# One attention and feed-forward block: K's and Q's weight blocks loaded together, in another order

## The chip, the cores and the metric

The kernel runs on one core of a Trainium2 chip. The metric is the time of the program on the device in microseconds (us): the median of 3 runs before the change. A profile of one execution stands beside it.

The engines are named as in the profile: PE is TensorE (matrix products), PEld its weight loads, DVE is VectorE, ACT is ScalarE, POOL is GpSimd, SP is SyncE. SP and ACT issue the DMAs of this kernel (SPq, ACTq).

## The reference

One input x of 2048 rows by 512 goes through a layer norm, and then through two branches whose results are added to x:

```python
def _A_ref(x, wqkv, wo):            # 32 heads of 16
    qkv = (x @ wqkv).reshape(B, S, 3, H, Dh).transpose(2, 0, 3, 1, 4)
    q, k, v = qkv[0], qkv[1], qkv[2]
    phi = lambda t: jnp.where(t > 0, t + 1, jnp.exp(t)) + 1e-6
    pq, pk = phi(q), phi(k)
    kv = jnp.einsum("bhsd,bhse->bhde", pk, v)
    z = jnp.einsum("bhsd->bhd", pk)
    num = jnp.einsum("bhqd,bhde->bhqe", pq, kv)
    den = jnp.einsum("bhqd,bhd->bhq", pq, z)[..., None] + 1e-6
    return (num / den).transpose(0, 2, 1, 3).reshape(B, S, D) @ wo

def _B_ref(x, w_gate, w_up, w_down):  # F = 1792
    return (silu(x @ w_gate) * (x @ w_up)) @ w_down

xn = layernorm(x)
return x + _A_ref(xn, A_wqkv, A_wo) + _B_ref(xn, B_w_gate, B_w_up, B_w_down)
```

All tensors are bfloat16. `A_wqkv` is 512 by 1536: in each row stand 512 columns for Q, then 512 for K, then 512 for V, that is 3 KB.

## The kernel before

The 2048 rows are 16 tiles of 128 (t = 0 to 15), and the 512 columns are four blocks of 128 (c = 0 to 3, `NDC`). A projection of one tile is four products that add into one PSUM bank, one for each block c; it needs x's tile transposed and block c of the weight matrix (128 rows, 512 columns, 128 KB).

The order of the work is written out by hand. `_Prog` keeps a list of operations for each engine in the order in which they are recorded, and puts a semaphore wait ahead of an operation only where another engine or a DMA has to be waited for. Each engine works through its list in order, and SP and ACT issue the DMAs in the order of their lists. Nothing is rearranged later.

The stages are:

1. **Start (about the first 11 us).** PE runs products on constants (`fill`, L271) until x tile 0 is there. For tiles 0 to 3, x less its mean (`xc_sb`) is transposed without waiting for the standard deviation, whose inverse is put in afterwards as a scale when ACT reads the product. VectorE makes the statistics (`bns`, L299, then `agg`, L302) and subtracts the mean (L380, L426); PE transposes (L410, L444; the transposes of tile 3 are a DMA, L435); ACT and VectorE copy the results into `xcT` (L419, L421, L456). Then `proj_part` (L499) makes one product of one block at a time for tiles 0 and 1, for K (`"wk"`) and Q (`"wq"`), and `proj_first` (L486) does two blocks at a time for tiles 2 and 3. ACT evacuates K with `first_ek` (L556, exp) and `first_pk` (L562, relu), and Q with `first_pq` (L574). GpSimd adds the two K parts of tile 0 (`feat_pool`, L581).
2. **K, Q and the state (to about 47 us).** For each further tile: K and Q projection (L472), then four products of `gtacc` (L624), which add pk's products with the normalised x into four banks.
3. **The feed-forward (to about 208 us).** 56 steps of gate and up products (L821), with the 16 output tiles (L1015, L1026) among them. An output tile is added to x on VectorE (L1039) and stored by SP (L1043).

Of the loads: `xload(eng, h, t0, n)` (L206) loads n tiles of x from tile t0, `wqkv_load` (L213) loads n blocks of one of the three matrices. The rows of the first `NLONE` = 6 tiles are taken as they stand (a tile is 128 consecutive rows); the other ten tiles share their rows so that partition p holds ten consecutive rows and two tiles are loaded as one piece of 2 KB a partition. The mapping also holds for the stores. A tile's rows of x and its rows of the output are the same, and no other step depends on which rows a tile has.

In the start `proj_part` is called in this order, where 0 and 1 are tiles, and the number behind the name is the block:

```python
# K: tile 0: blocks 0, 1, 3, 2; then tile 1: blocks 0, 1, 3, 2
# Q: tile 1: blocks 0, 1; tile 0: blocks 0, 1
#    (four transposes of tile 2)
# Q: block 2 of tile 0, of tile 1; block 3 of tile 0, of tile 1
```

Of the kernel before, what the change touches and what calls it, by code (L numbers as in the profile page):

```python
# [10 lines left out]
P = 128  # L11
S = 2048
D = 512
# [96 lines left out]
def bass_parallel_sum__linear_attn_block__swiglu_ffn__prompt_kernel(  # L110
# [12 lines left out]
    K = _Prog()  # L123
    pe, act, dve, pool, sp = nc.tensor, nc.scalar, nc.vector, nc.gpsimd, nc.sync
    bf, f32 = dt.bfloat16, dt.float32

    with contextlib.ExitStack() as es:
        E = es.enter_context

        def sb(name, shape, d=bf):  # L130
            return E(nc.sbuf_tensor(name, [P] + shape, d))
# [7 lines left out]
        wqkv_sb = sb("wqkv_sb", [NDC, 3 * D])  # L139
# [16 lines left out]
        warm = sb("warm", [1], f32)  # L156
# [35 lines left out]
        def bk(i):  # L192
            return ("bank", i)

        NLONE = 6

        def rows(v, t0, n):
            if t0 < NLONE:  # L200
                return v[t0 * P:(t0 + n) * P, :].rearrange("(t p) d -> p t d", p=P)
            return v[NLONE * P:, :].rearrange("(p t) d -> p t d", t=NT - NLONE)[:, t0 - NLONE:t0 - NLONE + n, :]

        def xload(eng, h, t0, n, after=()):
            K.dma(
                eng, lambda: h.dma_start(x_sb[:, t0:t0 + n, :], rows(xin, t0, n)),  # L206
                r=list(after), w=[("x", t0 + i) for i in range(n)],
            )

        def wqkv_load(eng, h, name, i, c0, n, after=()):  # L210
            K.dma(
                eng,
                lambda: h.dma_start(  # L213
                    wqkv_sb[:, c0:c0 + n, i * D:(i + 1) * D],
                    A_wqkv[c0 * P:(c0 + n) * P, i * D:(i + 1) * D].rearrange("(c p) f -> p c f", p=P),
                ),
                r=list(after), w=[(name, c) for c in range(c0, c0 + n)],
            )

        def wload(eng, h, name, dst, src):  # L220
# [28 lines left out]

        xload("sp", sp, 0, 1)  # L250
        wqkv_load("sp", sp, "wk", 1, 0, 2)
        wqkv_load("act", act, "wk", 1, 3, 1)
        wqkv_load("sp", sp, "wk", 1, 2, 1)
        xload("sp", sp, 2, 1)
        wqkv_load("sp", sp, "wq", 0, 0, 1)
        wqkv_load("sp", sp, "wq", 0, 1, 1)
        xload("sp", sp, 3, 1)
        wqkv_load("sp", sp, "wq", 0, 2, 1)
        wqkv_load("sp", sp, "wq", 0, 3, 1)
        xload("sp", sp, 4, 1)  # L260
        xload("sp", sp, 5, 1)
        xload("sp", sp, 6, 2)

        cw = nc.const_aps.tensor(1.0, (P, P), bf)
# [33 lines left out]
        def bns(t):  # L298
            K.op("dve", lambda: dve.bn_stats(stats[:, t, :], x_sb[:, t, :]), r=[("x", t)], w=[("st", t)])  # L299

        def agg(t):
            K.op("dve", lambda: dve.bn_aggr(mv[:, t, :], stats[:, t, :]), r=[("st", t)], w=[("mv", t)])  # L302
# [129 lines left out]
        def transpose_xc(t):  # L432
            K.dma(
                "sp",
                lambda: sp.dma_start_transpose(out=xcT[:, NDC * t:NDC * (t + 1), :], in_=xc_sb[:, t, :]),  # L435
                r=[("xc", t, 0), ("xc", t, 1)], w=[("xcT", t, c) for c in range(NDC)],
            )
# [43 lines left out]
        def proj_first(t, wname, h):  # L481
            lo, b = (D, kb(t)) if wname == "wk" else (0, qb(t))
            K.op(
                "pe",
                [
                    (lambda c=c: pe.matmul(  # L486
                        banks[b], xcT[:, NDC * t + c, :], wqkv_sb[:, c, lo:lo + D],
                        start=(c == 0), stop=(c == NDC - 1),
                    ))
                    for c in (2 * h, 2 * h + 1)  # L490
                ],
                r=[("xcT", t, i) for i in (2 * h, 2 * h + 1)] + [(wname, i) for i in (2 * h, 2 * h + 1)], w=[bk(b)],
            )

        def proj_part(t, wname, c, pos):
            lo, b = (D, kb(t)) if wname == "wk" else (0, qb(t))
            K.op(
                "pe",
                lambda: pe.matmul(  # L499
                    banks[b], xcT[:, NDC * t + c, :], wqkv_sb[:, c, lo:lo + D],  # L500
                    start=(pos == 0), stop=(pos == NDC - 1),
                ),
                r=[("xcT", t, c), (wname, c)], w=[bk(b)],
            )

        def kb(t):
            return 2 * (t % 2)

        def qb(t):
            return 2 * (t % 2) + 1  # L510
# [43 lines left out]
        def first_ek(t):  # L554
            K.op(
                "act", lambda: act.activation(ek[:, t % NE, :], banks[kb(t)], ACT.Exp, scale=rstd[:, t:t + 1]),  # L556
                r=[bk(kb(t)), ("rstd", t)], w=[("ek", t % NE)],
            )

        def first_pk(t):  # L560
            K.op(
                "act", lambda: act.activation(kpos[:, t % NE, :], banks[kb(t)], ACT.Relu, scale=rstd[:, t:t + 1]),  # L562
                r=[bk(kb(t)), ("rstd", t)], w=[("kpos", t % NE)],
            )
# [7 lines left out]
        def first_pq(t):  # L572
            K.op(
                "act", lambda: act.activation(pkq[:, t, 1, :], banks[qb(t)], ACT.Identity, scale=rstd[:, t:t + 1]),  # L574
                r=[bk(qb(t)), ("rstd", t)], w=[("pq", t)],
            )
# [96 lines left out]
        agg(3)  # L673
        proj_part(0, "wk", 0, 0)
        proj_part(0, "wk", 1, 1)
        proj_part(0, "wk", 3, 2)
        proj_part(0, "wk", 2, 3)
        first_ek(0)
        clip_k(0)
        xc_full(3)  # L680
        bns(4)
        proj_part(1, "wk", 0, 0)
        proj_part(1, "wk", 1, 1)
        proj_part(1, "wk", 3, 2)
        proj_part(1, "wk", 2, 3)
        proj_part(1, "wq", 0, 0)
        proj_part(1, "wq", 1, 1)
        transpose_xc(3)
        xload("sp", sp, 8, 2)
        xload("sp", sp, 10, 2)  # L690
        proj_part(0, "wq", 0, 0)
        proj_part(0, "wq", 1, 1)
        first_pk(0)
        tp_first(2, 0, 4)
        tc_first(2, 0, 4)
# [4 lines left out]
        agg(5)  # L700
        bns(6)
        agg(6)
        proj_part(0, "wq", 2, 2)
        proj_part(1, "wq", 2, 2)
        proj_part(0, "wq", 3, 3)
        first_pq(0)
        proj_part(1, "wq", 3, 3)
        proj_first(2, "wk", 0)
        proj_first(2, "wk", 1)
        eps_two(1, "pool")  # L710
# [413 lines left out]
```

## Time and profile before

| what | value |
|---|---|
| median of 3 runs | 210.15 us (209.99 to 210.45) |
| profiled execution | 210.88 us |
| its span, from the first instruction to the last | 209.6 us |
| PE busy | 206.9 us (99%) |
| DVE, ACT, POOL busy | 120.3, 71.3, 72.0 us |
| DMA traffic | 16.84 MB, mean 80 GB/s |

The profiled execution is one execution with the profiler on; times within it are microseconds from the start of its span. In the timeline a row gives the start, the length, the engine, the line, the operation with what it writes and reads, and how many instructions were merged. A row for a DMA on SPq or ACTq is the issuing of it, not the transfer. In brackets stands how long the engine had been idle, and what ended that. PE's products are pipelined: each is shown with its whole way through the array, so successive rows overlap.

### The profile page before, as it was taken

To read this page: it belongs to the slowest core of one execution; us is meant where nothing else is said; L and a number is where in the kernel's file an instruction comes from. 1 tells how busy PE (TensorE), PEld (TensorE's weight loads), DVE (VectorE), ACT (ScalarE), POOL (GpSimd) and SP (SyncE) were. 2 spreads that over 40 slices of the span, in tenths; PEclk is the share of its full clock that TensorE was granted. 3 is DMA by queue.
4 is the path that set the end of the run, shared out by engine and by line. 5 is a ranking of instruction groups with operands and counts; after the bars stand their busy time and mean duration, and the time that the engine had idled before them with its cause. 6 is when DMAs were issued, how large, how long until landed. Compare 5 with 4: busy or idle time off the path is not lost.

```text
span 209.6 us, 2822 instructions
## 1 busy us (share of the span) xinstructions
PE 206.9 (99%) x1014; PEld 94.5 (45%) x1014; DVE 120.3 (57%) x246; ACT 71.3 (34%) x126; POOL 72.0 (34%) x90
## 2 busy tenths in 40 slices
PE   8999999999999999999999999999999999999996
PEld 3444444444444444444444444444444444444444
DVE  4989989335465874637355746365556535374122
ACT  6686666976543331302122312213031213121000
POOL 3526977658032443223141422240424132221200
DMA  6763644697797021010101110102011010110101
GB/s 201 225 179 71 127 78 100 175 377 240 192 359 68 2 46 26 29 25 25 50 2 50 28 25 25 50 0 53 2 48 25 27 28 25 46 32 25 50 28 50
DMA packets 30287, 16.84 MB, mean 80 GB/s; under 512 B 20928, under 2 KB 29632, under 8 KB 30272
## 3 DMA queue, kind: packets, MB, share of 16 engines
q1 hardware_dynamic: 29984, 16.39, 29.9%
q10 hardware_dynamic: 288, 0.26, 0.4%
q8 instruction: 8, 0.13, 0.3%
q14 instruction: 7, 0.06, 0.1%
HBM read 9.70 MB, written 2.10 MB: 56 GB/s over the span
## 4 chain that ended last, share of the span: by engine, by line
PE 97%; DMA 1%; DVE 1%; issue 0%
PE psum L821 46%; PE psum L1026 23%; PE psum L472 10%; PE psum L1015 7%; PE psum L624 7%; PE psum L499 2%; PE psum L486 2%; DMA x_sb<-in_A_x_dram 1%; PE psum L444 0%; DVE stats L299 0%; PE psum L928 0%; PE psum L410 0%; PE psum L951 0%; DVE xc_sb L380 0%; DVE out_sb L1039 0%
## 5 line engine op out<-in xcount | busy, mean ns | idle before, releaser
L836 ACT ACTIVATE sg<-psum 128x512 bf16<-128x512 f32 x56 | 33.4, 598 | 106.0 <-PE psum L821 103.6
L821 PE MATMUL psum<-xnT,wg_sb 128*128 128x512 bf16 x224 | 57.5, 379 | 0.0
L821 PE MATMUL psum<-xnT,wu_sb 128*128 128x512 bf16 x224 | 57.5, 379 | 0.0
L970 POOL TENSOR_TENSOR prod<-pkq,zb 128x512 f32<-128x512 bf16 x16 | 18.6, 1161 | 55.9 <-DVE pkq L548 55.9
L821 PEld LDWEIGHTS psum<-xnT,wu_sb 128*128 128x128 bf16 x224 | 21.9, 98 | 26.4
L821 PEld LDWEIGHTS psum<-xnT,wg_sb 128*128 128x128 bf16 x224 | 21.7, 98 | 26.2 <-issue 0.2
L1039 DVE TENSOR_TENSOR out_sb<-psum,x_sb 128x512 bf16<-128x512 f32 (+2 forms) x17 | 11.2, 660 | 35.9 <-PE psum L1026 35.9
L994 POOL TENSOR_TENSOR pqn<-pkq,rden 128x512 bf16<-128x512 bf16 x16 | 16.9, 1055 | 36.6 <-DVE rden L988 36.6
L842 DVE TENSOR_TENSOR pkq<-psum,sg 128x512 bf16<-128x512 f32 x28 | 19.2, 686 | 17.1 <-PE psum L821 14.7
L842 DVE TENSOR_TENSOR xn_sb<-psum,sg 128x512 bf16<-128x512 f32 x28 | 18.8, 671 | 14.2 <-PE psum L821 13.6
L1026 PE MATMUL psum<-wd_sb,xn_sb 128*128 128x512 bf16 (+2 forms) x126 | 25.7, 355 | 0.0
L1026 PE MATMUL psum<-wd_sb,pkq 128*128 128x512 bf16 x112 | 25.5, 379 | 0.0
L472 PE MATMUL psum<-wqkv_sb,xnT 128*128 128x512 bf16 x96 | 22.5, 379 | 0.0
L616 POOL TENSOR_TENSOR zacc<-zacc,pkq 128x512 f32<-128x512 f32 x15 | 17.3, 1155 | 5.0 <-DVE ek L539 4.6
L1026 PEld LDWEIGHTS psum<-wd_sb,xn_sb 128*128 128x128 bf16 x126 | 11.8, 98 | 12.5
L1026 PEld LDWEIGHTS psum<-wd_sb,pkq 128*128 128x128 bf16 x112 | 11.0, 98 | 13.2
L1015 PE MATMUL psum<-m_sb,eq 128*128 128x512 bf16 (+2 forms) x68 | 16.6, 366 | 0.0
L624 PE MATMUL psum<-pkq,xn_sb 128*128 128x512 bf16 x64 | 15.9, 379 | 0.0
L472 PEld LDWEIGHTS psum<-wqkv_sb,xnT 128*128 128x128 bf16 x96 | 9.4, 98 | 11.3
L978 DVE TENSOR_REDUCE den<-prod 128x32 f32<-128x512 f32 x16 | 10.9, 683 | 5.9 <-POOL prod L970 5.9
L299 DVE BATCH_NORM_STATS2 stats<-x_sb 128x6 f32<-128x512 bf16 x16 | 10.9, 679 | 3.3 <-DMA x_sb<-in_A_x_dram 3.3
L548 DVE SCALAR_TENSOR_TENSOR pkq<-pkq,eq 128x512 bf16<-128x512 bf16 x16 | 11.1, 693 | 0.6
(73 smaller groups left out, 139.3 us busy)
## 6 DMA issues: line engine op xcount, KB each, us to landing
out_dram<-out_sb SPq DMA_DIRECT2D x15, 128.0 KB, 1.7
wg_sb<-in_B_w_gate_dram SPq DMA_DIRECT2D x2, 896.0 KB, 8.2
wu_sb<-in_B_w_up_dram SPq DMA_DIRECT2D x2, 896.0 KB, 6.4
wd_sb<-in_B_w_down_dram SPq DMA_DIRECT2D x1, 1792.0 KB, 11.1
x_sb<-in_A_x_dram SPq DMA_DIRECT2D x5, 256.0 KB, 3.0
x_sb<-in_A_x_dram SPq DMA_DIRECT2D x5, 128.0 KB, 3.2
wqkv_sb<-in_A_wqkv_dram SPq DMA_DIRECT2D x5, 128.0 KB, 3.4
wqkv_sb<-in_A_wqkv_dram SPq DMA_DIRECT2D x1, 512.0 KB, 8.4
```

Of the source, the lines that this page charges most:

```text
L472: (lambda c=c: pe.matmul(banks[b], xnT[:, c, t * P:(t + 1) * P], wqkv_sb[:, c, lo:lo + D], start=(c == 0), stop=(c == NDC - 1),))
L548: lambda: dve.scalar_tensor_tensor(out=dst, in0=src, scalar=0.0, in1=e, op0=ALU.max, op1=ALU.add,),
L616: lambda: pool.tensor_tensor(out=zacc[:, :], in0=zacc[:, :], in1=pk, op=ALU.add),
L624: (lambda c=c: pe.matmul(banks[4 + c], xn_sb[:, t, c * P:(c + 1) * P], pkq[:, t, 0, :], start=(t == 0), stop=(t == NT - 1),))
L821: (lambda c=c: pe.matmul(banks[b], w_sb[:, c, fc * P:(fc + 1) * P], xnT[:, c, C * 512:(C + 1) * 512], start=(c == 0), stop=(c == NDC - 1),))
L836: lambda: act.activation(sg[:, j % NSG, :], banks[gb], ACT.Silu),
L842: lambda: dve.tensor_tensor(out=hT(C, fc), in0=banks[ub], in1=sg[:, j % NSG, :], op=ALU.mult,),
L970: lambda: pool.tensor_tensor(out=p, in0=pkq[:, t, 1, :], in1=zb[:, :], op=ALU.mult),
L994: lambda: pool.tensor_tensor(out=pqn[:, t % NPN, :].rearrange("p (i g h e) -> p g i h e", i=NB, g=NG, e=DH), in0=pkq[:, t, 1, :].rearrange ...
L1015: (lambda g=g: pe.matmul(dst, pqnT(t)[:, g, :], m_sb[:, g, lo:hi], start=(g == 0), stop=False,))
L1026: (lambda fc=fc: pe.matmul(dst, hT(C, fc)[:, jj * P:(jj + 1) * P], wd_sb[:, fc, lo:hi], start=False, stop=(fc == NFC - 1),))
L1039: lambda: dve.tensor_tensor(out=o, in0=src, in1=x_sb[:, t, lo:hi], op=ALU.add),
```

## The change

- K's blocks 2 and 3 are no longer loaded alone. `qk_load` loads block c of Q and of K together: in each row of `A_wqkv` these are 1024 neighbouring columns, 2 KB. It is called for blocks 2 and 3.
- Q's blocks 0 and 1 come in one load, behind x tile 3.
- x tile 2 is issued on ACT rather than on SP. It waits for the warm-up activation (`warm`). K's block 3, which ACT issued, is now part of SP's second joint load.
- `NLONE` is 4: x tiles 4 and 5 come in one load of 2 KB pieces, and tiles 4 to 15 share their rows in twelves.
- The products of tiles 0 and 1 follow the new order of the blocks.

```diff
-        NLONE = 6
+        NLONE = 4
...
+        def qk_load(eng, h, c):
+            K.dma(
+                eng,
+                lambda: h.dma_start(wqkv_sb[:, c, 0:2 * D], A_wqkv[c * P:(c + 1) * P, 0:2 * D]),
+                w=[("wk", c), ("wq", c)],
+            )
...
         xload("sp", sp, 0, 1)
         wqkv_load("sp", sp, "wk", 1, 0, 2)
-        wqkv_load("act", act, "wk", 1, 3, 1)
-        wqkv_load("sp", sp, "wk", 1, 2, 1)
-        xload("sp", sp, 2, 1)
-        wqkv_load("sp", sp, "wq", 0, 0, 1)
-        wqkv_load("sp", sp, "wq", 0, 1, 1)
+        xload("act", act, 2, 1, [("warm",)])
+        qk_load("sp", sp, 2)
+        qk_load("sp", sp, 3)
         xload("sp", sp, 3, 1)
-        wqkv_load("sp", sp, "wq", 0, 2, 1)
-        wqkv_load("sp", sp, "wq", 0, 3, 1)
-        xload("sp", sp, 4, 1)
-        xload("sp", sp, 5, 1)
+        wqkv_load("sp", sp, "wq", 0, 0, 2)
+        xload("sp", sp, 4, 2)
         xload("sp", sp, 6, 2)
...
         proj_part(0, "wk", 0, 0)
         proj_part(0, "wk", 1, 1)
-        proj_part(0, "wk", 3, 2)
-        proj_part(0, "wk", 2, 3)
+        proj_part(0, "wk", 2, 2)
+        proj_part(1, "wk", 0, 0)
+        proj_part(1, "wk", 1, 1)
+        proj_part(0, "wk", 3, 3)
+        proj_part(1, "wk", 2, 2)
+        proj_part(1, "wk", 3, 3)
         first_ek(0)
         clip_k(0)
         xc_full(3)
         bns(4)
-        proj_part(1, "wk", 0, 0)
-        proj_part(1, "wk", 1, 1)
-        proj_part(1, "wk", 3, 2)
-        proj_part(1, "wk", 2, 3)
-        proj_part(1, "wq", 0, 0)
-        proj_part(1, "wq", 1, 1)
+        proj_part(0, "wq", 2, 0)
+        proj_part(0, "wq", 3, 1)
...
-        proj_part(0, "wq", 0, 0)
-        proj_part(0, "wq", 1, 1)
+        proj_part(1, "wq", 2, 0)
+        proj_part(1, "wq", 3, 1)
         first_pk(0)
...
-        proj_part(0, "wq", 2, 2)
-        proj_part(1, "wq", 2, 2)
-        proj_part(0, "wq", 3, 3)
+        proj_part(0, "wq", 0, 2)
+        proj_part(0, "wq", 1, 3)
+        proj_part(1, "wq", 0, 2)
         first_pq(0)
-        proj_part(1, "wq", 3, 3)
+        proj_part(1, "wq", 1, 3)
```

The last argument of `proj_part` is the product's place among its four (the first clears the bank, the last closes the sum).

## The prediction

> **What bounds the kernel now.** I read the page first, then TensorE's share by stage, then the chain of waits over the first 12 us, and last the timeline of that stretch. On the page:
>
> ```profile
> span 209.6 us, 2822 instructions
> ...
> PE 206.9 (99%) x1014; PEld 94.5 (45%) x1014; DVE 120.3 (57%) x246; ACT 71.3 (34%) x126; POOL 72.0 (34%) x90
> ...
> PE 97%; DMA 1%; DVE 1%; issue 0%
> ```
>
> The span is TensorE (PE) work. Busy time by windows (length, then busy time of PE, PEld and the others) says where it isn't:
>
> ```profile
> 11.20:47.60 36.40, 36.40 (x171) 16.51 (x169) 27.02 (x64) 26.16 (x48) 24.64 (x36) 1.00 0.63 163
> 47.60:207.80 160.20, 160.18 (x803) 73.45 (x801) 85.31 (x158) 37.65 (x63) 42.44 (x40) 1.00 0.21 53
> 207.80:209.60 1.80, 0.00 (x0) 0.00 (x0) 0.29 (x1) 0.00 (x0) 0.00 (x0) 1.00 0.25 73
> ```
>
> From 11.2 to 207.8 us PE is full: 0.02 us idle in 196.6. The last 1.8 us are the last store. So only the start is left, which is where the change works. The chain of waits there and PE's rows of the timeline (start, length):
>
> ```profile
> 0.80 2.15 DMA x_sb<-in_A_x_dram
> ...
> 4.26 0.40 PE psum L410 x2
> ```
> ```profile
> 5.09 3.52 PE L499 MATMUL psum<-wqkv_sb,xcT 128*128 128x512 bf16 x12
> 8.45 0.39 PE L444 MATMUL psum<-ident,xc_sb 128*128 128x128 bf16 x4
> 8.67 1.03 PE L499 MATMUL psum<-wqkv_sb,xcT 128*128 128x512 bf16 x4
> ```
>
> PE's first useful work, at 4.26, follows x tile 0 through VectorE; the change touches nothing on that path. From then on PE's rows follow one another without idle time: **no product waits for a weight block in this trace.** What is slow is the rate. Weight loads (PEld) inside the first twelve products:
>
> ```profile
> 5.95 0.15 PEld L499 LDWEIGHTS psum<-wqkv_sb,xcT 128*128 128x128 bf16 x1 [0.28 <-issue]
> 6.37 0.15 PEld L499 LDWEIGHTS psum<-wqkv_sb,xcT 128*128 128x128 bf16 x1 [0.27 <-issue]
> 6.72 1.39 PEld L499 LDWEIGHTS psum<-wqkv_sb,xcT 128*128 128x128 bf16 x7 [0.20 <-issue]
> ```
>
> Products start 0.42 us apart up to 6.37, 0.35 apart once, then 1.39 / 7 or about 0.2 apart (the twelve take 8.45 - 5.09 = 3.36). PE runs at half rate until about 6.6 us. Of twelve products 3.6 are at half rate and cost 3.6 x 0.21 = 0.77 us more than at full rate.
>
> **Where the weights stand against their use.** Issues on SP and ScalarE (SPq, ACTq), ScalarE's warm-up and the first copy of x tile 0 for PE, then the answers of the DMA view in narrow windows round single issues (KB, us from issue to landing):
>
> ```profile
> 1.10 0.42 ACTq L206 DMA_DIRECT2D x_sb<-in_A_x_dram  x1
> ...
> 1.26 0.93 SPq L213 DMA_DIRECT2D wqkv_sb<-in_A_wqkv_dram  x2
> ...
> 2.09 0.20 ACT L236 ACTIVATE warm<-warm 128x1 f32<-128x1 f32 x1
> ...
> 4.12 0.94 SPq L213 DMA_DIRECT2D wqkv_sb<-in_A_wqkv_dram  x2
> ...
> 4.59 0.23 DVE L421 COPY xcT<-psum 128x128 bf16<-128x128 bf16 x1
> ```
> ```profile
> wqkv_sb<-in_A_wqkv_dram SPq DMA_DIRECT2D x1, 256.0 KB, 3.0
> x_sb<-in_A_x_dram ACTq DMA_DIRECT2D x1, 128.0 KB, 2.2
> ...
> wqkv_sb<-in_A_wqkv_dram SPq DMA_DIRECT2D x1, 128.0 KB, 3.4
> ```
> ```profile
> wqkv_sb<-in_A_wqkv_dram SPq DMA_DIRECT2D x1, 128.0 KB, 3.6
> ```
> ```profile
> wqkv_sb<-in_A_wqkv_dram SPq DMA_DIRECT2D x2, 128.0 KB, 3.7
> ```
> ```profile
> xcT<-xc_sb SPq DMA_TRANSPOSE x1, 2.5
> ```
>
> K blocks 0 and 1 land at 1.26 + 3.0 = 4.3, used at 5.09. K block 2 is issued at 1.73 and lands at 1.73 + 3.4 = 5.1. Q block 2 lands at 4.12 + 3.6 = 7.7 and is used at 8.67: 0.95 us to spare. Q block 3 lands at 4.59 + 3.7 = 8.3 and is used by the third product of that group, 8.67 + 0.43 = 9.1: 0.8 to spare. These are the narrowest of the weights.
>
> **Fewer, larger loads.** Four issues go, all on SP; ACT has as many as before (x 2 in place of K block 3). An issue is 0.93 / 2 = 0.47 us of SP, and SP computes nothing, so this only brings the later loads forward. Landing in the new order is set by bytes in line. By 5.1 us the old order has landed x 0, x 1 and K's four blocks, 768 KB; the new one has x 0, x 1, K 0 and 1, and the joint K/Q block 2, also 768 KB, with x 2 (128 KB) beside it on the other queue. The rate, last column in GB/s:
>
> ```profile
> 5.00:6.00 1.00, 1.00 (x6) 0.45 (x5) 1.00 (x4) 0.84 (x3) 0.02 (x1) 1.00 1.05 356
> 6.00:6.90 0.90, 0.90 (x4) 0.35 (x3) 0.83 (x4) 0.00 (x0) 0.20 (x1) 1.00 0.94 162
> ```
>
> At 356 GB/s 128 KB take 0.37 us. So K/Q block 2 lands between 5.1 (x 2 later) and 5.5 (x 2 before it); K/Q block 3, 0.74 later, at 5.85 to 6.25; x 3 at 6.2 to 6.6; Q 0 and 1 at 6.95 to 7.35; x 4 and 5 at 7.7 to 8.1. I keep 1 KB rates for the 2 KB pieces; no row ahead of 7 us has 2 KB pieces, and if they are faster these ends come down. The lull of the second row (162 GB/s, engines busy) costs 0.9 x (1 - 162/356) = 0.5 us once; it may fall on any of these loads.
>
> **The new product order.** The twelve products keep their places, of which the times are known. K 2 is the third, 5.95: 0.45 to 0.85 us to spare. K 3 moves from third to sixth place, 6.72 + 0.2 = 6.9: 0.65 to 1.05 to spare. Q 2 is ninth, about 7.6, and came with K 2. Q 0 and 1 come at 8.67 with at least 1.3. Even with the lull in the worst place each is covered. Cost 0, gain 0: a wait that isn't there can't be removed.
>
> **What hangs on K's first result.** Tile 0's K is complete after the sixth product rather than the fourth, 2 x 0.216 = 0.43 us later. Behind it:
>
> ```profile
> 6.92 0.69 ACT L556 ACTIVATE ek<-psum,rstd 128x512 bf16<-128x512 f32 x1 [1.08 <-PE psum L499]
> ...
> 7.50 0.68 ACT L562 ACTIVATE kpos<-psum,rstd 128x512 f32<-128x512 f32 x1
> ...
> 8.28 1.16 POOL L581 TENSOR_TENSOR pkq<-kpos,ek 128x512 bf16<-128x512 f32 x1 [0.45 <-ACT kpos L562]
> 8.42 1.28 SPq L435 DMA_TRANSPOSE xcT<-xc_sb  x1
> ...
> 8.69 0.69 DVE L299 BATCH_NORM_STATS2 stats<-x_sb 128x6 f32<-128x512 bf16 x1 [0.30 <-DMA x_sb<-in_A_x_dram]
> 8.76 0.66 ACT L456 ACTIVATE xcT<-psum 128x256 bf16<-128x256 bf16 x2 [0.57 <-PE psum L444]
> ...
> 11.26 1.03 PE L624 MATMUL psum<-pkq,xn_sb 128*128 128x512 bf16 x4
> ...
> 12.12 1.89 PE L486 MATMUL psum<-wqkv_sb,xcT 128*128 128x512 bf16 x8
> ```
>
> ACT was idle 0.57 before the copies at 8.76; with ek at 7.35 and kpos at 7.93 to 8.61 it still reaches them in time, by 0.15. GpSimd's sum then ends at 8.28 + 1.16 + 0.43 = 9.9, wanted at 11.26. VectorE's clip and x 3's subtraction, 0.43 later at most, eat the 0.30 it spent waiting for x 4, which now lands before 8.1. SP's transpose of x 3 (8.42) and the two x loads behind it slip by under 0.43; its product is at 12.12, and the transpose, 2.5 us in the row above, lands by 8.85 + 2.5 = 11.35. Nothing reaches PE.
>
> **x 2 on ACT.** It waits for the warm-up's end, 2.29, and the next on that queue is the mean of x 1, which waits for x 1 (1.10 + 2.2 = 3.3); an issue of 0.47 fits. It lands 2.2 to 3.4 after 2.3, at 4.5 to 5.7. VectorE asks for it here:
>
> ```profile
> 5.74 0.66 DVE L299 BATCH_NORM_STATS2 stats<-x_sb 128x6 f32<-128x512 bf16 x1
> ...
> 6.65 0.48 DVE L380 TENSOR_SCALAR xc_sb<-x_sb,mv 128x256 bf16<-128x256 bf16 x2
> ```
>
> In time at either end; and the transposes that use it are at 8.45, 1.3 us after 7.13. The Trainium skill (DMA: Bandwidth & Descriptors, "Rules for kernel authors") speaks against this part: spreading DMAs over queues doesn't add bandwidth, as they interleave on the same engines. By that, x 2 delays K/Q block 2 by its share, the 5.5 above; the sum stays.
>
> **Rows 512 to 2047 in twelves.** Tiles 4 and 5 become strided, and the stride of the later tiles goes from 10 to 12 KB. The stores, from the page:
>
> ```profile
> out_dram<-out_sb SPq DMA_DIRECT2D x15, 128.0 KB, 1.7
> ```
>
> Only the last store counts: 1.8 - 0.29 (VectorE) = 1.5 us of the end, against this median of 1.7 over contiguous and strided ones. No row has a 12 KB stride: I bound it at 0.2 either way and take 0, as the 1.7 holds both kinds.
>
> **Sum.** 209.6 + 0 = 209.6 us of span; the execution was 210.88, so 1.28 lies around it. The median of the runs shown, 210.15, is 0.73 below the profiled execution. If what lies around the span is the same there, PE in such a run is 0.73 ahead at the end, which is what half rate costs in the first twelve products (0.77). Then Q block 3 is wanted at 9.1 - 0.73 = 8.37 and lands at 8.3: the before is at the edge of a wait that the new order has not. I take 0.1 for that: **210.05 us**, own range 209.75 to 210.5 (0.4 down; the scatter of the runs up).
>
> **Rivals.**
> *The clock comes up earlier in most runs and the before does wait for Q.* PE can lead the trace by at most 0.77 + 0.27 (its first product can't start before tile 0's first copy, 4.59 + 0.23 = 4.82, against 5.09). Q 3 is then wanted at 8.06, 0.25 before it lands; with a second lull, 0.75. The change takes that away: 209.9 without the lull, still inside the forecast, and 209.4 with it. For: the 0.73. Against: the trace has no such wait. The Trainium skill (TensorE: Matmul & The Clock Gate, Part 1) says that the window which opens the clock is free-running, so the moment varies from run to run; only one run here shows it. Chance of over 0.2% (about what a measurement of this kernel can tell from no change, 0.42 us): 0.28.
> *K block 3 comes too late: slower.* With the clock up early K 3 is wanted at about 6.0 (6.9 less 0.77 to 1.04) instead of 6.9, and it now has 1152 KB ahead of and in it instead of 640. If the lull falls before it, 6.25 + 0.5 = 6.75, PE waits 0.6 to 0.85, and as PE is full behind, nothing gives that back: 210.75 to 211.0 against 210.15, or 0.1 to 0.25 less where Q's own wait goes with it. It decides from a landing after 6.0 (early clock) or 6.9 (late). Against: lull and early clock must meet, and the before has a like exposure later. Chance 0.22.
> *The change does nothing*, as PE never waited in either: 210.15, inside the forecast. With it, no change: 0.50.
>
> **Range.** 209.5 to 210.75 leaves out the ends of both rivals.
>
> **What would show it.** Right: in the changed kernel's trace PE without idle time from 4.26, and as many products at half rate as its clock's moment makes; Q 0 and 1 landed by 7.9; no wait for x 4 on VectorE; ek at about 7.35. Wrong: a PEld or PE wait for a wqkv load among the first sixteen products, a stall at ACT's copies at 8.76, or a last stage unlike 1.8 us.

## The result and the profile after

The changed kernel takes 211.22 us (median of 15 runs, 210.79 to 213.17) against 210.43 (15 runs, 209.99 to 210.76): a ratio of 1.0053, 95% interval 1.0032 to 1.0074 (the ratio is not that of the two medians, which lie 0.79 apart). It is slower by about 0.8 to 1.1 us, outside the forecast's range. The profiled execution took 211.46 with a span of 210.2, so 1.26 lies around the span, as before.

On the page of the changed kernel PE's busy time is 0.5 us less than before and the span is 0.6 more:

```profile
span 210.2 us, 2818 instructions
...
PE 206.4 (98%) x1014; PEld 94.1 (45%) x1014; DVE 120.1 (57%) x246; ACT 71.2 (34%) x126; POOL 71.9 (34%) x90
...
PE 96%; DMA 2%; SPq 0%; issue 0%; DVE 0%
```

The windows answer for the later stages and the tail (length, then busy time of PE and the others, or of PE alone in the last row) shows nothing new there: PE is as full as it was, and the tail is 1.8 us again.

```profile
12.70:47.60 34.90, 34.90 (x163) 15.86 (x163) 26.61 (x63) 24.97 (x46) 23.86 (x36) 1.00 0.65 166
48.20:208.40 160.20, 160.19 (x803) 73.52 (x801) 85.31 (x158) 37.65 (x63) 42.47 (x40) 1.00 0.21 53
```
```profile
208.40:210.20 1.80, 0.00 (x0) 1.00 0.25 73
```

So the loss is made before 12.7 us. The timeline there (in brackets the idle time and what ended it; L502 are the products on single blocks, L302 the statistics, L429 the subtraction for x 3, L438 its transpose, L489 the products of tiles 2 and 3):

```profile
1.72 0.93 SPq L223 DMA_DIRECT2D wqkv_sb<-in_A_wqkv_dram  x2
2.33 0.33 ACTq L206 DMA_DIRECT2D x_sb<-in_A_x_dram  x1
...
5.15 0.59 PE L502 MATMUL psum<-wqkv_sb,xcT 128*128 128x512 bf16 x2
...
6.80 2.34 PE L502 MATMUL psum<-wqkv_sb,xcT 128*128 128x512 bf16 x10 [1.05 <-DMA wqkv_sb<-in_A_wqkv_dram]
7.36 0.70 DVE L302 BATCH_NORM_STATS2 stats<-x_sb 128x6 f32<-128x512 bf16 x1 [1.47 <-DMA x_sb<-in_A_x_dram]
...
9.70 0.35 DVE L429 TENSOR_SCALAR xc_sb<-x_sb,mv 128x512 bf16<-128x512 bf16 x1
...
10.07 1.29 SPq L438 DMA_TRANSPOSE xcT<-xc_sb  x1
...
11.79 1.03 PE L627 MATMUL psum<-pkq,xn_sb 128*128 128x512 bf16 x4
...
12.73 0.59 PE L489 MATMUL psum<-wqkv_sb,xcT 128*128 128x512 bf16 x2
```

The DMA view of the three loads concerned (last column: us from issue to landing; the first is K/Q block 2, the second block 3, the third x 2):

```profile
wqkv_sb<-in_A_wqkv_dram SPq DMA_DIRECT2D x1, 256.0 KB, 4.9
```
```profile
wqkv_sb<-in_A_wqkv_dram SPq DMA_DIRECT2D x1, 256.0 KB, 5.2
x_sb<-in_A_x_dram ACTq DMA_DIRECT2D x1, 128.0 KB, 5.0
```

Two waits are new. **PE waits 1.05 us for K/Q block 2**, which lands at 6.66. **VectorE waits 1.47 us for x 2**, which lands at 7.33 instead of 5.42. VectorE works in order, so x 3's statistics, the clip of tile 0 and x 3's subtraction come late too; x 3's transpose is issued at 10.07 instead of 8.42 and lands at 12.59, and tile 3's first product starts at 12.73 instead of 12.12. The four products ahead of it, 0.22 apart from 11.79, would have let it start at 12.65. The gap is so small that PE's row shows no idle time, because a product's row is 0.38 us long while the starts are 0.22 apart; it shows only in the starts. The chain of waits therefore passes over it and names the louder wait, that for K/Q block 2:

```profile
1.72 4.94 DMA wqkv_sb<-in_A_wqkv_dram
...
6.80 2.34 PE psum L502 x10
```

Which of the two makes the loss is the question of the experiments. PE in this execution was at full rate from its first product (5.15, 5.37: 0.22 apart), against about 6.6 us before. The trace of before lost 0.77 us to its half rate, so the two traces set side by side understate what the change costs. (The profile's clock column reads 1.00 in both, so PE's rate is read from the starts alone.)

### The profile page after: what moved, and what is told of

Same layout as the page of the kernel before. It is cut to its first block, busy times and chain, and to the rows that moved or that the text cites. A ratio compares the mean times of both kernels' runs of the same rounds, so it can differ in the third digit from the quotient of the medians.

```text
span 210.2 us, 2818 instructions
## 1 busy us (share of the span) xinstructions
PE 206.4 (98%) x1014; PEld 94.1 (45%) x1014; DVE 120.1 (57%) x246; ACT 71.2 (34%) x126; POOL 71.9 (34%) x90
## 4 chain that ended last, share of the span: by engine, by line
PE 96%; DMA 2%; SPq 0%; issue 0%; DVE 0%
PE psum L824 46%; PE psum L1029 23%; PE psum L475 10%; PE psum L1018 7%; PE psum L627 7%; DMA wqkv_sb<-in_A_wqkv_dram 2%; PE psum L489 2%; PE psum L502 2%; PE psum L931 0%; SPq L213 0%; SPq L206 0%; PE psum L954 0%; DVE out_sb L1042 0%; PE psum L447 0%
## 5 line engine op out<-in xcount | busy, mean ns | idle before, releaser
L981 DVE TENSOR_REDUCE den<-prod 128x32 f32<-128x512 f32 x16 | 10.9, 684 | 5.9 <-POOL prod L973 5.9
L302 DVE BATCH_NORM_STATS2 stats<-x_sb 128x6 f32<-128x512 bf16 x16 | 10.9, 680 | 4.5 <-DMA x_sb<-in_A_x_dram 4.5
```

## The experiments

Each ratio is to the kernel before on the same chip in the same set of runs (its median was 210.31 to 210.37). The first four runs set three theories on the late block against one another: P, the 2 KB pieces; L, a lull that hits whatever is in flight; X, x 2 on the second queue. The next four ask which wait costs: W, both; K, only the weights; V, only x 2 by way of VectorE.

**1. K apart from Q, 1 KB pieces.**

```diff
-        qk_load("sp", sp, 2)
-        qk_load("sp", sp, 3)
+        wqkv_load("sp", sp, "wk", 1, 2, 2)
+        wqkv_load("sp", sp, "wq", 0, 2, 2)
```

> The changed kernel, but K blocks 2 and 3 come in one 256 KB load of 1 KB pieces and Q blocks 2 and 3 in another, on the same queue and in the same places; the products keep the new order. As many bytes stand ahead of the third product as with the joint K/Q load. Theory P (the 2 KB pieces of the joint load start slowly): K 2 lands at about 5.2 us instead of 6.66, PE has no 1.05 us wait, the time is within 0.3 us of the kernel before. Theory L (256 KB in one load behind a lull that hits whatever is in flight at 3.5 to 4.5 us): K 2 lands after 6 us and the time stays 0.6 to 1.0 us above the kernel before. Theory X (x 2 on ScalarE's queue takes the rate): lands at about 5.5, 0 to 0.4 us above.

210.58, ratio 1.0014 (1.0000 to 1.0028). K 2 and 3 land at 5.86, not at 5.2, and PE, at full rate early, waits 0.34 us. But x 2 moved as well: it lands at 6.11. Nothing is decided for P, since two things changed at once.

**2. x 2 on SP behind the joint loads.**

```diff
-        xload("act", act, 2, 1, [("warm",)])
         qk_load("sp", sp, 2)
         qk_load("sp", sp, 3)
+        xload("sp", sp, 2, 1)
```

> The changed kernel, but x 2 is issued on SP behind the two joint loads instead of on ScalarE's queue. Theory X (the second queue's packets hold up K/Q block 2): K/Q block 2 lands before 5.5 us, no wait of PE, within 0.3 us of the kernel before. Theories P and L: K/Q block 2 lands as late as in the changed kernel (about 6.6), 0.6 to 1.0 us above the kernel before.

210.97, ratio 1.0032 (1.0019 to 1.0045). Block 2 lands at 6.16 and x 2 at 7.16. Theory X falls: with x 2 off the second queue the joint load is still later than 5.5, and x 2 is as late as on ScalarE's queue.

**3. The new rows and x 4 and 5 in one load, nothing else.**

```diff
-        NLONE = 6
+        NLONE = 4
-        xload("sp", sp, 4, 1)
-        xload("sp", sp, 5, 1)
+        xload("sp", sp, 4, 2)
```

> The kernel before with only the new row mapping (tiles 4 to 15 in twelves) and x 4 and 5 in one load. All three theories: the time of the kernel before within 0.2 us, and no wait of VectorE for x 4. If the mapping itself costs something (loads or stores at a 12 KB stride): 0.3 us or more above it, with longer landings of x or of the last store.

210.68, ratio 1.0014 (1.0004 to 1.0025), 0.3 us, which no theory had. Its timeline shows VectorE waiting for x 4, which now lands together with x 5 at 9.2:

```profile
9.21 0.69 DVE L298 BATCH_NORM_STATS2 stats<-x_sb 128x6 f32<-128x512 bf16 x1 [0.91 <-DMA x_sb<-in_A_x_dram]
```

**4. Four products ahead of block 2 instead of two.**

```diff
-        proj_part(0, "wk", 2, 2)
         proj_part(1, "wk", 0, 0)
         proj_part(1, "wk", 1, 1)
+        proj_part(0, "wk", 2, 2)
         proj_part(0, "wk", 3, 3)
```

> The changed kernel, but tile 1's products on K blocks 0 and 1 stand ahead of tile 0's on block 2, so that four products instead of two cover the wait for K/Q block 2. All theories: two products of 0.216 us at full rate less to wait, 0.4 us below the changed kernel, 0.2 to 0.6 above the kernel before. If the late block 3 (7.41 us) decides in its place, under 0.2 us is gained.

211.28, ratio 1.0043 (1.0030 to 1.0057): no gain that can be told. In its trace block 2 lands at 4.99, and PE works through its twelve products without idle time, though at half rate until about 7.0 us. The loss is there all the same, and the x 2 rows remain to explain its last part:

```profile
5.02 3.75 PE L502 MATMUL psum<-wqkv_sb,xcT 128*128 128x512 bf16 x12
7.26 0.69 DVE L302 BATCH_NORM_STATS2 stats<-x_sb 128x6 f32<-128x512 bf16 x1 [1.52 <-DMA x_sb<-in_A_x_dram]
...
9.97 1.28 SPq L438 DMA_TRANSPOSE xcT<-xc_sb  x1
11.46 1.03 PE L627 MATMUL psum<-pkq,xn_sb 128*128 128x512 bf16 x4
12.61 1.67 PE L489 MATMUL psum<-wqkv_sb,xcT 128*128 128x512 bf16 x7
```

Four products 0.22 apart from 11.46 would let the next start at 12.32. It starts at 12.61, after x 3's transpose has landed (12.47).

**5. x 2 early.**

```diff
-        xload("act", act, 2, 1, [("warm",)])
+        xload("act", act, 2, 1)
```

> The changed kernel, but x 2 is issued on ScalarE right behind x 1, without the wait for the warm-up (at about 1.5 us instead of 2.3). Theory W (two waits: PE for K/Q block 2, and VectorE for x 2, which lands in the order of issue over both queues and so behind both joint loads): x 2 lands by 5.4 us instead of 7.3, VectorE does not wait 1.5 us for it, the wait of PE before tile 3's products goes; K/Q block 2 is as late as before or 0.3 later; 0.3 to 0.6 us above the kernel before. Rival K (only the weights' lateness counts): 0.7 to 1.1 above. Rival V (only x 2 counts): within 0.2.

210.66, ratio 1.0021 (1.0010 to 1.0031): as theory W has it, 0.6 us of the loss is gone. x 2 lands at 5.78 and VectorE doesn't wait for it. PE's wait for block 2 is still there; tile 3's first product starts at 12.03, 0.7 earlier:

```profile
6.20 2.32 PE L502 MATMUL psum<-wqkv_sb,xcT 128*128 128x512 bf16 x10 [0.53 <-DMA wqkv_sb<-in_A_wqkv_dram]
...
8.56 1.28 SPq L438 DMA_TRANSPOSE xcT<-xc_sb  x1
...
12.03 1.89 PE L489 MATMUL psum<-wqkv_sb,xcT 128*128 128x512 bf16 x7
```

**6. x 2 late in the kernel before.** Here everything else, weights, pieces, rows and products, is as before.

```diff
-        xload("sp", sp, 2, 1)
         wqkv_load("sp", sp, "wq", 0, 0, 1)
         wqkv_load("sp", sp, "wq", 0, 1, 1)
         xload("sp", sp, 3, 1)
         wqkv_load("sp", sp, "wq", 0, 2, 1)
+        xload("sp", sp, 2, 1)
```

> The kernel before with only x 2 moved, on SP, behind Q block 2; weights, pieces, rows and products as they were. x 2 lands at 7.2 to 7.8 us as in the changed kernel, every weight at its old time or earlier. Theory W: VectorE waits 1.5 to 2 us for x 2, x 3's transpose is issued at about 10 instead of 8.4, PE waits ahead of tile 3's products; 0.2 to 0.6 us above the kernel before. Rival K: within 0.2. Rival V: 0.7 to 1.1 above.

211.61, ratio 1.0065 (1.0052 to 1.0077), so x 2 alone costs as much as the whole change or more. That is above what even rival V had, and far above K's nothing. x 2 lands at 7.90, 0.57 later than in the changed kernel's trace, which accounts for part of that; VectorE's wait, the transpose and tile 3's product follow:

```profile
7.92 0.69 DVE L299 BATCH_NORM_STATS2 stats<-x_sb 128x6 f32<-128x512 bf16 x1 [2.15 <-DMA x_sb<-in_A_x_dram]
9.22 0.48 PE L444 MATMUL psum<-ident,xc_sb 128*128 128x128 bf16 x4 [0.86 <-DVE xc_sb L380]
...
10.64 1.28 SPq L435 DMA_TRANSPOSE xcT<-xc_sb  x1
...
13.27 1.02 PE L486 MATMUL psum<-wqkv_sb,xcT 128*128 128x512 bf16 x3
```

**7. Both taken away.** Experiments 1 and 5 together.

> The changed kernel with both: K blocks 2 and 3 in one load of 1 KB pieces, Q blocks 2 and 3 in another, and x 2 issued on ScalarE right behind x 1. Theory W: neither wait is left but up to 0.4 us on K blocks 2 and 3 with an early clock; within 0.3 us of the kernel before, and not above K and Q apart with the late x 2 (210.58 against 210.37). Rivals K and V: the same, since both lates are taken away.

210.58, ratio 1.0018 (1.0003 to 1.0032). x 2 lands at 5.45, K 2 and 3 at 5.82, and PE has no wait among its first twelve products. It can't be told from experiment 1, nor from experiment 5.

**8. The changed kernel once more.**

> The changed kernel once more, for a second trace. All theories: 0.5 to 1.1 us above the kernel before; x 2 lands within 0.4 us of K/Q block 3. Theory P (2 KB pieces always start slowly): K/Q block 2 lands at 6.0 or later again. If slow packets fall on the joint loads by chance: anywhere from 5.0 to 6.7.

211.25, ratio 1.0055 (1.0036 to 1.0073). In this trace block 2 lands at 5.17 and block 3 at 6.88, so theory P is out: the 2 KB pieces can start as fast as any. For the weights something like theory L is left, a lateness that falls on one block or the other from trace to trace; none of the three theories had x 2 on VectorE. PE waits for block 3 instead, 0.59 us, and the end is again set by x 2:

```profile
6.92 1.69 PE L502 MATMUL psum<-wqkv_sb,xcT 128*128 128x512 bf16 x7 [0.59 <-DMA wqkv_sb<-in_A_wqkv_dram]
7.07 0.69 DVE L302 BATCH_NORM_STATS2 stats<-x_sb 128x6 f32<-128x512 bf16 x1 [1.28 <-DMA x_sb<-in_A_x_dram]
...
9.79 1.28 SPq L438 DMA_TRANSPOSE xcT<-xc_sb  x1
```

**9 and 10. The rows as before.** Experiment 5 (joint loads) and experiment 7 (K and Q apart), each with this edit:

```diff
-        NLONE = 4
+        NLONE = 6
-        xload("sp", sp, 4, 2)
+        xload("sp", sp, 4, 1)
+        xload("sp", sp, 5, 1)
```

> The changed kernel with x 2 issued on ScalarE right behind x 1, and with the rows as before (six plain tiles, x 4 and x 5 each in a load of its own). The joint K/Q loads and the new product order stay. If the remainder of 0.3 us that an early x 2 left comes from x 4 (landing only together with x 5) or from the mapping: within 0.15 us of the kernel before. If it comes from the joint loads: 0.2 to 0.4 above.

> As the one above, but K blocks 2 and 3 in one load of 1 KB pieces and Q blocks 2 and 3 in another. If pieces of 2 KB are no slower than pieces of 1 KB: the same as the one above within 0.2 us. If they are: 0.2 to 0.4 below it. In both cases x 4 lands before 8.4 us, and VectorE waits less for it than in the kernel before.

210.76, ratio 1.0019 (1.0005 to 1.0033), and 210.52, ratio 1.0010 (0.9999 to 1.0022). With the joint loads the rows make no difference (1.0021 before), so what an early x 2 leaves over belongs to the weights: PE waits 1.02 us for block 2 in the trace of experiment 9 and nothing in that of experiment 10. The two ratios overlap, so this is the traces' word and not the medians'. The row of experiment 9:

```profile
6.39 2.32 PE L503 MATMUL psum<-wqkv_sb,xcT 128*128 128x512 bf16 x10 [1.02 <-DMA wqkv_sb<-in_A_wqkv_dram]
```

**11. Only the mapping of the rows** (`NLONE = 4`, x 4 and x 5 in single loads).

> The kernel before with only the mapping of the rows (tiles 4 to 15 in twelves); x 4 and x 5 are loaded one by one, now in strided 1 KB pieces. If the 12 KB stride costs: 0.3 us above the kernel before, as with x 4 and 5 in one load (210.68 against 210.37). If it is x 4's waiting for x 5: within 0.15 us.

210.36, ratio 0.9999 (0.9985 to 1.0012). A 12 KB stride costs nothing that can be told. What experiment 3 adds to this kernel is the joint load alone, so its 0.3 us go to x 4's waiting for x 5, as its trace had it.

**12. Q's blocks in pairs in the kernel before** (blocks 0 and 1 in one load, 2 and 3 in another, at their places).

> The kernel before with Q blocks 0 and 1 in one load and 2 and 3 in another, at their places, two issues fewer on SP; nothing else. If SP's issues (0.47 us for 128 KB) hold the loads behind 6 us: Q 2 and 3 and x 4 come 0.3 to 0.6 us earlier, VectorE no longer waits for x 4, and the time is 0 to 0.3 us below the kernel before. If the transfers themselves are the limit: no change, or up to 0.2 above, as block 0 waits for block 1.

210.46, ratio 1.0008 (0.9993 to 1.0022). Two issues fewer bring nothing; in its trace PE waits 0.25 us for the pair of blocks 0 and 1. None of the twelve is faster than the kernel before.

**What sets the end.** From the start of tile 3's first product to PE's last there are 195.66 us in every trace but that of experiment 3 (196.04, where PE waits for VectorE after it), and the tail adds 1.84. So the time hangs on when that product starts. Sorted by x 2's landing, one trace to a kernel (the kernel before was caught 0.45 above its median, with PE's rate late), all in us from the start of the span:

| kernel | x 2 lands | K 2 usable | K 3 usable | x 3's transpose lands | tile 3's first product | span |
|---|---|---|---|---|---|---|
| before | 5.42 | 5.10 | 4.91 | 10.91 | 12.12 | 209.6 |
| 7: K and Q apart, x 2 early | 5.45 | 5.82 | 5.82 | 10.95 | 11.81 | 209.3 |
| 9: x 2 early, rows as before | 5.61 | 6.25 | 6.92 | 11.26 | 12.22 | 209.7 |
| 5: x 2 early | 5.78 | 6.06 | 6.73 | 11.06 | 12.03 | 209.5 |
| 1: K and Q apart | 6.11 | 5.86 | 5.86 | 11.35 | 11.83 | 209.3 |
| 8: changed, again | 7.05 | 5.17 | 6.88 | 12.29 | 12.43 | 209.9 |
| 2: x 2 on SP, behind | 7.16 | 6.16 | 6.83 | 12.42 | 12.55 | 210.0 |
| 4: other order | 7.23 | 4.99 | 7.04 | 12.47 | 12.61 | 210.1 |
| changed | 7.33 | 6.66 | 7.41 | 12.59 | 12.73 | 210.2 |
| 6: x 2 late in the kernel before | 7.90 | 5.17 | 4.97 | 13.13 | 13.27 | 210.8 |

In the last five rows the transpose lands 5.23 to 5.26 after x 2, the product starts 0.13 or 0.14 after that, and the span is x 2's landing plus 202.88, within 0.02. The trace has PE waiting there for the transpose's semaphore. K 2 differs by 1.7 us among these rows, and PE reached full rate at moments from about 4.3 to 7.0 us; neither shows in the span. In the first five rows the transpose is there about 0.5 us or more ahead of the product, and PE's own pace (its rate, and the waits for weights) decides. So it does in the four traces left out of the table (experiments 3, 10, 11 and 12: the product at 11.36, 11.53, 11.22 and 11.61, the transpose at 10.84, 10.82, 11.08 and 11.27); in that of experiment 11 the two meet.

How much x 2 adds to PE's own pace differs. Four products 0.22 apart would have let tile 3's product start 0.28 to 0.30 earlier in experiments 2, 4, 6 and 8 (in experiment 6 x 2 had held PE up once before, 0.86 at tile 2's transposes), but only 0.08 earlier in the changed kernel's own trace: there block 2's wait had made PE nearly as late, and by this sum either delay alone would have cost about as much.

## Why the prediction was wrong

**What held.** The start was the only place; the later stages, the tail and the 1.26 around the span stayed. SP's issues came as forecast (1.72 for block 2). The mapping of the rows costs nothing that can be told (experiment 11). PE does reach full rate at different moments: ahead of 4.3 us in five of the fourteen traces, at about 7.0 in the latest (experiment 4, where the products start 0.43 apart up to 6.72). The Trainium skill (TensorE: Matmul & The Clock Gate, Part 1) puts the varying moment down to a free-running window. The traces agree that the moment varies; they don't show the window.

**The step that failed: x 2 on ACT.** It was put at 4.5 to 5.7, by the two latencies of ScalarE's queue in the trace of before (2.2 and 3.4). Those loads had fewer bytes ahead of them. In these traces a load's place in line followed from its moment of issue, whichever of the two queues it was on. Moved from 2.23 on SP to 2.33 on ACT, x 2 kept its moment, but the loads issued before it had grown by 256 KB, from K's two blocks to two joint blocks. The DMA view's queue rows for the changed kernel, in windows of 2.9 to 3.6, 3.6 to 4.6, 4.6 to 6.6 and 6.6 to 7.4 us (q1 is SP's queue, q10 ACT's; packets, MB, share of the engines' time; the four packets of q10 in the first window are x 1's last):

```profile
q1 hardware_dynamic: 230, 0.23, 113.4%
q10 hardware_dynamic: 4, 0.00, 0.7%
```
```profile
q1 hardware_dynamic: 92, 0.17, 101.4%
```
```profile
q1 hardware_dynamic: 340, 0.47, 67.4%
q10 hardware_dynamic: 141, 0.13, 18.7%
```
```profile
q1 hardware_dynamic: 261, 0.31, 105.8%
q10 hardware_dynamic: 3, 0.00, 0.8%
```

x 2 moves nothing until 4.6; then 141 of its 144 packets start within 2 us, and the last three soon after 6.6. Its semaphore counts sixteen parts, the first at 5.71 and the last at 7.33, and VectorE waits for the last. By the prediction's own figures, x 2 behind both blocks would have been put at 6.2 to 6.6 (block 3 at 5.85 to 6.25, and 0.37 for 128 KB), or 6.7 to 7.1 with the lull; it landed at 7.33 here and at 7.05 in experiment 8.

The page of the Trainium skill that the prediction named (DMA: Bandwidth & Descriptors, "Rules for kernel authors") says that DMAs spread over queues run on the same engines and interleave, without more bandwidth. The trace agrees that ACT's queue gave x 2 no rate of its own, but up to 4.6 us it shows no interleaving: SP's queue moved 0.23 MB between 2.9 and 3.6, and x 2 nothing. The prediction applied the rule to what x 2 would do to block 2, and not to what the blocks would do to x 2.

**The second failure is in the same part:** "in time at either end", with 1.3 us to spare at tile 2's transposes on PE. That follows x 2 to its direct reader, but not VectorE's list behind the waiting instruction: x 3's statistics, the clip, x 3's subtraction, then a DMA transpose. That chain stands in the prediction, under the heading before, priced against K's first result; its slack, 12.12 - 10.9 = 1.2 us, was there to be set against x 2 as well. By the table x 2 could land no later than 12.12 - 5.24 - 0.13 = 6.75 in that trace, and earlier than that when PE is at full rate early; even the top of the forecast's range, 5.7, was near it then.

**The weights.** Block 2 was put at 5.1 to 5.5 and landed at 6.66, 5.17, 6.16 and 4.99 in the four traces with x 2 late (the changed kernel's two and experiments 2 and 4); block 3 was put at 5.85 to 6.25, or 6.75 with the lull, and landed at 6.8 to 7.4. In each of the four traces block 3 came over 0.5 us after the end of its forecast without the lull. "Even with the lull in the worst place each is covered" missed by a little in the prediction's own figures too: block 2 at 5.5 and 0.5 of lull make 6.0, and it was wanted at 5.95. The lull was priced (0.5) as something that might fall on any load; in the changed kernel's own trace it fell on block 2: 0.17 MB in the 1.0 us above, engines busy throughout. The rival "K block 3 comes too late", 210.75 to 211.0, named a wait that does occur (0.59 us in experiment 8), but not the one that ends last. With x 2 in time a wait for the weights is what is left (for block 2, 0.53 and 1.02 us in the traces of experiments 5 and 9, both 0.2% in time); where x 2 is late it adds nothing to the span.

**x 4** was to land at 7.7 to 8.1; it landed at 9.13, and VectorE's not waiting for it was only because VectorE itself was late (9.96 instead of 8.69). **The 0.1 us of gain** for Q's edge can't be told behind the loss. The edge itself exists: in experiment 3's trace, with the weights as before and PE early, PE's weight load waits 0.22 us for Q block 2, which lands at 7.85. The 0.73 us by which the prediction had a usual run ahead of the trace came from three runs; by the median of fifteen, 210.43, it is 0.45.

Open: why the DMA engines are slow at certain moments, from 3.6 us in the changed kernel's trace and from 6 us in that of the kernel before, and so why block 2 lands anywhere in 1.7 us. In the changed kernel's trace nine 2 KB packets that start between 3.59 and 4.24 take 0.69 to 1.38 us each, where the median around them is 0.08; what holds them isn't shown. Open too is the spread of the changed kernel's runs, up to 213.17 where the fifteen of the kernel before end at 210.76. By the table's sum that would be x 2 landing at about 9.0 (an estimate); no trace was taken of such a run.

## What to carry to other kernels

When a load is moved to another queue, take its landing from all bytes issued before it on any queue, as these traces have it, and not from that queue's latency. When a load may come late, follow the in-order list of the engine that waits for it to the end, DMAs included, and compare with the slack of whatever hangs there. The loudest wait need not be the one that costs: find the instruction from which the rest is rigid, and ask what starts it.

## What the runs showed of the hardware

- A load on ACT's queue did not pass the loads issued before it on SP's. In the nine traces of the table in which ACT issued x 2 or K 3, it landed in the order of issue over both queues, but for loads issued 0.1 us apart, which came out either way (x 2 at 7.33 beside 7.41, 7.23 beside 7.04, 6.11 beside 6.56).
- The same 256 KB load, issued at 1.72 or 1.73 us, landed anywhere from 4.99 to 6.66 us. Pieces of 2 KB made no difference that these runs can tell: in the changed kernel's trace the median packet of 2 KB took 84 ns and that of 1 KB 46 ns, about the same for each byte.
